# Row maxima written over their scores, score passes that share four banks, and a new order of work in an attention and GEGLU kernel

## The chip, the cores and the metric

The kernel runs on one core of one Trainium2 chip. The metric is the device time of one execution in microseconds, as the median of three runs. The engines are TensorE (PE), VectorE (DVE), ScalarE (ACT), GpSimd (POOL) and the queue of SyncE (SP), which issues all transfers.

## The reference

The input x has 2048 rows of 512. A layer norm, then attention with 32 heads of 16 in four segments of 512 rows, with a compressive memory that is carried from one segment to the next; then a second layer norm and a gated feed-forward with 1376 columns. Cut to what matters:

```python
for s in range(4):                                   # segments of 512 rows
    logits = einsum("bhqd,bhkd->bhqk", qs, ks) * scale + mask
    p = softmax(logits);  a_dot = p @ vs             # mask: -1e9 where the key stands behind the query
    a_mem = (phi(qs) @ M) / (phi(qs) @ z + 1e-6)
    outs.append(g * a_mem + (1 - g) * a_dot)         # g = sigmoid(beta)
    M += phi(ks).T @ vs;  z += phi(ks).sum(rows)
h   = x + concat(outs) @ wo
out = h + (gelu(ln(h) @ w_gate) * (ln(h) @ w_up)) @ w_down
```

All in fp32. The projections are done as three products of high and low parts (`SPLIT`), the softmax with the maximum of each row.

## The kernel before

The order of the work is not that of the Python code. Every instruction is recorded with an engine, a duration, a due time and the values that it reads and writes (`Sched.op`), and `Sched.run` then picks one after another: of those that could start first by its constants, the one with the least due time. `DUE` (L34) holds offsets to the due times, found by a search. `LAT` (L126) is what the planner believes of the time from one engine's result to another's start, `TAKEN` (L132) of the time until a buffer is free. `Pool_` (L54) is a set of buffers; with `fifo` they are given out in the order in which they were asked for, and `then` names the pool that takes them over when nobody waits any more. What the planner picks is fixed in each engine's program; at run time only semaphores hold an instruction back.

The stages are: a prologue (layer norm of the first segments, splitting of weights, the first projections), attention in 16 units of eight heads and one segment, and the feed-forward stage. Each unit is two half units Q of four heads, 32 in all. For each half unit:

- `qkv` (L664) projects q and k (`project`, L610: 4 x 3 products, the low part of xt used by the second of each three), splits them into high and low parts `hl`, and sends these by DMA into the stacked tiles `stq` and `stk`. `phi` (L624) makes `pq` and `pk` for the memory.
- `pass_a` (L785) is for the row maxima. It makes scores with queries on the partitions, for four blocks of 128 queries: 512 and 384 columns (one head to a bank, the wide ones), 256 (two heads to a bank) and 128 (four heads to a bank, the narrow ones). VectorE adds the mask and reduces each head (L807); the elementwise result isn't needed and went to one of two buffers `junk`, the maximum goes to `nm`. The maxima are split in two parts (L823, L826), transposed on PE (L830), copied to `mx` (L833) and sent by DMA into `stq`.
- `pass_b` (L837) makes the scores again with keys on the partitions and the maximum subtracted by the extra rows (L862, L869), takes exp on ScalarE (L876) into `pt`, masks on GpSimd (L879), and accumulates the attention output on PE (L900).

There are eight PSUM banks of 512 columns: three for general use (`PD`), two for the scores of pass A (`PA`), two for those of pass B (`PB`), and one for the accumulation (`PPV`). In the feed-forward stage the last five become `PX` and `PYZ`.

In the prologue `layer_norm` (L455) with `done` keeps PE busy with 17 transposes whose result nobody reads (L497), then transposes the normalised rows (L568) and splits them into high and low parts of xt (L588 on ScalarE, L589 on VectorE). The first unit's two projections are two calls of `project`.

Of the kernel before, what the change touches and what calls it, by code (L numbers as in the profile page):

```python
# [31 lines left out]


DUE = {  # L34
# [17 lines left out]
}  # L52


# [65 lines left out]
class Op:  # L120
# [2 lines left out]

LAT = {  # L126
    "PE": {"PE": 0.0, "ACT": 0.27, "DVE": 0.246, "POOL": 0.24, "SP": 0.25},
    "ACT": {"PE": 0.14, "ACT": 0.12, "DVE": 0.137, "POOL": 0.172, "SP": 0.12},
    "DVE": {"PE": 0.108, "ACT": 0.12, "DVE": 0.17, "POOL": 0.165, "SP": 0.12},
    "POOL": {"PE": 0.085, "ACT": 0.08, "DVE": 0.09, "POOL": 0.12, "SP": 0.12},  # L130
}
TAKEN = {"PE": 0.22, "ACT": 0.14, "DVE": 0.12, "POOL": 0.1}  # L132
DRAIN = 0.1


# [106 lines left out]
def infini_geglu(ctx: ExitStack, tc: tile.TileContext, x, wq, wk, wv, wo, beta,  # L242
# [8 lines left out]
    def sb(name, shape, dt=F32):  # L251
        return p0.tile(shape, dt, name=name)
# [17 lines left out]
        return S.op("POOL", dur, prio, fn, ins, outs, **k)  # L270

    def dma(prio, fn, ins, outs, kb=256, dur=None, **k):
        return S.op("SP", dur or (0.4 if kb == 256 else 0.68), prio, fn, ins, outs, lat=kb / 290, **k)

    def mm(n):
        return max(n / 2400 + 0.0133, 0.109)
# [5 lines left out]
    PD = Pool_(banks[0:3])  # L282
    PX = Pool_([], fifo=True)
    PYZ = Pool_([], fifo=True)
    PA = Pool_(banks[3:5], then=PX)
    PB = Pool_(banks[5:7], then=PYZ)
    PPV = Pool_(banks[7:8], then=PYZ)

    def slots(name, n):
# [21 lines left out]
    PACC = Pool_([], fifo=True)  # L311
    PGE = Pool_(many("ge", 1, [P, D]))
    PC = Pool_([])
    PPT = Pool_(many("pt", 2, [P, D]), then=PACC)
    PROW1 = Pool_(many("pt1", 9, [P, D]), then=PPT)
    PJ = Pool_(many("junk", 2, [P, D]), then=PC)
    PE_ = Pool_(many("e", 1, [P, D]), then=PC)
    PPQ = Pool_(many("pq", 1, [P, D]), then=PC)
    PPK = Pool_(many("pk", 1, [P, D]), then=PC)
    PPKN = Pool_(many("pkn", 1, [P, D]), then=PC)  # L320
    PPVS = Pool_(many("pvs", 1, [P, D]), then=PGE)
# [7 lines left out]
    PMB = Pool_(many("mb", 7, [P, 160]))  # L329
    PNM = Pool_(many("nm", 2, [P, 2, 2, 4]))  # L330
    PMM = Pool_(many("mm", 2, [P, 2, 2, 8], F32R))
    PMX = Pool_(many("mx", 2, [32, P]))
    PBN = Pool_(many("bn", 2, [P, 4, 6]))
    PMV = Pool_(many("mv", 2, [P, 4, 2]))
    PLN = Pool_(many("ln", 8, [P, 4]))

    ident = sb("ident", [P, P])
    amask = sb("amask", [P, D])
# [1 line left out]
    one = sb("one", [P, 1])  # L340
    gt = sb("gt", [P, 2, NCH])
    tick = sb("tick", [P, 1])
    o_dram = dram.tile([NSEG, 4, P, NCH, P], F32, name="o_dram")
    r_dram = dram.tile([16, 2, 8, D], F32, name="r_dram")
    pv_dram = dram.tile([16, 2, P, D], F32, name="pv_dram")
# [2 lines left out]
    vident, vamask, vmmask, vgt = (Val() for _ in range(4))  # L348


    vh = Val(PJ)
    vj = Val(PJ)


# [101 lines left out]
    def layer_norm(prio, rows, dst, off=False, keep=None, acq=None, done=(), behind=(), scratch=None):  # L456
# [37 lines left out]
        if done and not behind:  # L494

            wm = Val(PB)
            pe(17 * 0.227, prio, lambda: [nc.tensor.transpose(  # L497
                wm.t[0:24, 0:P], bn.t.rearrange("p t k -> p (t k)"), ident) for n in range(17)],
                [bn, vident], [wm])

        def g():
# [62 lines left out]
                    op1=OP.mult), [rows[t], mv, y], [rows[t]])  # L564
        if done and not behind:

            pts = [Val(PA if dc == 3 else PD) for dc in range(ND)]
            pe(4 * TR, prio, lambda: [nc.tensor.transpose(  # L568
                pts[dc].t[:, t * P:(t + 1) * P], rows[t].t[:, dc * P:(dc + 1) * P], ident)
                for t in range(4) for dc in range(ND)], [*rows, vident], pts, acq=dst)  # L570
            for dc in range(ND):
                split_psum(prio, pts[dc], dst[dc])
            return
# [47 lines left out]
            pe(3 * mm(D), prio, f, [w, XT[s][dc]], [pm], acq=acq)  # L621
        return pm

    def phi(prio, pm, pool_):  # L624

        e, r = Val(PE_), Val(pool_)
        act(D, prio, lambda: nc.scalar.activation(e.t, pm.t, AF.Relu, scale=-1.0), [pm], [e],
            acq=[r])
        act(D, prio, lambda: nc.scalar.activation(e.t, e.t, AF.Exp, scale=-1.0), [e], [e],
            src=0.092)  # L630
        dve(D, prio, lambda: nc.vector.scalar_tensor_tensor(
            r.t, pm.t, 0.0, e.t, op0=OP.max, op1=OP.add), [pm, e], [r])
        return r
# [31 lines left out]
    def qkv(U):  # L665
# [5 lines left out]
        moved = prio + DUE["d"][U]  # L671
        for Q in half:
            STQ[Q], STK[Q] = Val(PSQ), Val(PSK)
        for i in range(2):
            hl = Val(PHL)
            if U == 0:
                HL0.append(hl)
            pm = project(first + 0.1 * i, W[s // 2, c, i], s, [hl])
            sc = 0.25 if i == 0 else 1.0
            act(D, first, lambda pm=pm, hl=hl, sc=sc: nc.scalar.activation(  # L680
                hl.t[:, 0], pm.t, AF.Copy, scale=sc), [pm], [hl])
            dve(D, first, lambda pm=pm, hl=hl, sc=sc: nc.vector.scalar_tensor_tensor(  # L682
                hl.t[:, 1], pm.t, sc, hl.t[:, 0].bitcast(F32), op0=OP.mult, op1=OP.subtract),
                [pm], [hl])
            if i == 0 and s:
                PQ[U] = phi(first, pm, PPQ)
            if i == 1 and s < NSEG - 1:
                PQ[U, "k"] = phi(first, pm, PPK)
# [94 lines left out]
    def pass_a(Q):  # L783
# [4 lines left out]
        def part(heads, i):  # L788
# [12 lines left out]
            m = mm(2 * w if i < 2 else w)  # L801
            pe(m * len(heads) / 2 if i < 2 else m, prio, f, [sq, sk], [sa], acq=[nm], tail=m)
            for k, (a, p) in enumerate(heads):
                junk = Val(PJ)

                def g(k=k, a=a, p=p, junk=junk):
                    nc.vector.tensor_tensor_reduce(  # L807
                        out=junk.t[:, :w], in0=sa.t[:, k * w:(k + 1) * w], in1=amask[:, D - w:],
                        op0=OP.add, op1=OP.min, scale=-1.0, scalar=BIG,
                        accum_out=nm.t[:, a, p, i:i + 1])  # L810
                dve(w, prio, g, [sa, vamask], [junk, nm], chain=True)
        for i in (3, 2):
            for n in range(4):
                part([(n % 2, n // 2)], i)
# [23 lines left out]
    def pass_b(Q):  # L838
# [55 lines left out]
        def accum(kbs, last):  # L894
            def f():
                for kb in kbs:
                    for n in range(4):
# [7 lines left out]
            pe(sum(0.02 + 0.86 * (4 - kb) / 4 for kb in kbs), Q + 1.122 + DUE["p"][Q], f,  # L905
               [va, *dict.fromkeys(pt[n, kb][0] for kb in kbs for n in range(4))], [pv], head=0.03,
               tail=0.02, mode="c")
        for n in range(4):
# [395 lines left out]
```

## Time and profile before

| | |
|---|---|
| median of 3 runs | 831.09 us (830.61 to 831.82) |
| the profiled execution | 830.79 us, span 829.1 us |
| PE busy | 805.0 us, 97% of the span |
| PE weight load busy | 623.6 us |
| DVE busy | 612.0 us, 74% |
| ACT busy | 563.5 us, 68% |
| POOL busy | 484.2 us, 58% |
| granted clock | 1.000 |

Busy time is the time in which at least one instruction of the engine was under way. Instructions overlap a little, and the ends of matmuls are modelled, so a busy PE is not one that gets all it could do; where it lost time is seen better from the starts of its instructions and from what released them. A row of a group gives busy time and mean duration, then the idle time before its instructions and what ended it. A row of the timeline gives the start, the duration and the instruction.

### The profile page before, as it was taken

To read this page: it belongs to the slowest core of one execution; us is meant where nothing else is said; L and a number is where in the kernel's file an instruction comes from. 1 tells how busy PE (TensorE), PEld (TensorE's weight loads), DVE (VectorE), ACT (ScalarE), POOL (GpSimd) and SP (SyncE) were. 2 spreads that over 40 slices of the span, in tenths; PEclk is the share of its full clock that TensorE was granted. 3 is DMA by queue.
4 is the path that set the end of the run, shared out by engine and by line. 5 is a ranking of instruction groups with operands and counts; after the bars stand their busy time and mean duration, and the time that the engine had idled before them with its cause. 6 is when DMAs were issued, how large, how long until landed. Compare 5 with 4: busy or idle time off the path is not lost.

```text
span 829.1 us, 15346 instructions
## 1 busy us (share of the span) xinstructions
PE 805.0 (97%) x4709; PEld 623.6 (75%) x4709; DVE 612.0 (74%) x1831; ACT 563.5 (68%) x1127; POOL 484.2 (58%) x719
## 2 busy tenths in 40 slices
PE   5999999999999999999999999999999999999998
PEld 4877767777777677776667677777888887788886
DVE  7888678788895878888896874676568856756565
ACT  6877868689988768776776862787467464545551
POOL 7533433444445444544736895788697686778750
PEclk9999999999999999999999999999999999999999
DMA  6543534565456564556554665531111341212102
GB/s 229 148 133 94 153 108 130 151 182 155 118 156 177 159 154 119 154 152 169 165 163 144 200 200 166 164 115 48 55 55 48 95 162 51 65 39 63 51 1 102
DMA packets 71750, 103.52 MB, mean 125 GB/s; under 512 B 14324, under 2 KB 24884, under 8 KB 71668
## 3 DMA queue, kind: packets, MB, share of 16 engines
q1 hardware_dynamic: 71668, 102.54, 42.6%
q8 instruction: 37, 0.61, 0.3%
q14 instruction: 45, 0.37, 0.2%
HBM read 54.92 MB, written 21.43 MB: 92 GB/s over the span
## 4 chain that ended last, share of the span: by engine, by line
PE 77%; DVE 10%; ACT 4%; issue 3%; POOL 3%; DMA 2%; SPq 1%; ACTq 0%; POOLq 0%; DVEq 0%
PE bank L1145 19%; PE bank L1206 14%; PE bank L619 8%; PE bank L797 8%; PE bank L869 7%; PE bank L900 7%; PE bank L973 4%; PE bank L648 4%; DVE junk L807 3%; ACT pt L876 1%; PE bank L726 1%; POOL raw L1122 1%; PE bank L772 1%; PE bank L579 1%; DVE hl L682 1%
## 5 line engine op out<-in xcount | busy, mean ns | idle before, releaser
L807 DVE CUSTOM_DVE_ANT_0 junk<-bank,amask 128x256 f32<-128x256 f32 (+3 forms) x512 | 228.3, 485 | 43.4 <-PE bank L797 40.3
L879 POOL TENSOR_SCALAR_AFFINE_SELECT pt<-pt 128x128 f32<-128x128 f32 (+2 forms) x352 | 118.8, 346 | 191.6 <-ACT pt L876 183.5
L876 ACT ACTIVATE pt<-bank 128x512 f32<-128x512 f32 (+1 forms) x352 | 181.4, 560 | 42.8 <-PE bank L869 36.4
L797 PE MATMUL bank<-stk,stq 128*128 128x512 f32 (+2 forms) x384 | 128.1, 377 | 4.3 <-DVE nm L807 3.9
L869 PE MATMUL bank<-stq,stk 128*128 128x384 f32 (+2 forms) x384 | 110.8, 351 | 1.7 <-ACT pt L876 1.4
L619 PE MATMUL bank<-xt,w 128*128 128x512 f32 x384 | 108.4, 394 | 1.1 <-DVE xt L589 1.1
L1211 DVE TENSOR_TENSOR pt<-pt,bank 128x512 f32<-128x512 f32 x96 | 65.0, 685 | 41.7 <-PE bank L1206 40.1
L797 PEld LDWEIGHTS bank<-stk,stq 128*128 128x128 f32 x384 | 68.6, 188 | 28.4 <-DVE nm L807 13.8
L869 PEld LDWEIGHTS bank<-stq,stk 128*128 128x128 f32 x384 | 67.3, 188 | 19.9 <-ACT pt L876 8.3
L619 PEld LDWEIGHTS bank<-xt,w 128*128 128x128 f32 x384 | 70.4, 188 | 12.5 <-DVE xt L589 1.3
L900 PE MATMUL bank<-pt,vaug 128*32 128x512 f32 (+3 forms) x1024 | 77.0, 436 | 0.0
L900 PEld LDWEIGHTS bank<-pt,vaug 128*32 128x32 f32 x1024 | 28.9, 109 | 39.1 <-issue 30.2
L648 PE MATMUL bank<-wv,xt 128*128 128x256 f32 x384 | 54.9, 283 | 0.0
L648 PEld LDWEIGHTS bank<-wv,xt 128*128 128x128 f32 x384 | 52.2, 189 | 1.8 <-issue 0.2
L1145 PE MATMUL bank<-xt,w 128*128 128x512 f32 (+1 forms) x186 | 51.2, 391 | 0.4 <-DVE n L1171 0.4
L1115 POOL TENSOR_TENSOR w<-raw,w 128x512 fp32r<-128x512 f32 (+3 forms) x37 | 42.0, 1137 | 6.8 <-ACT w L1113 6.6
L435 POOL TENSOR_TENSOR w<-raw,w 128x512 fp32r<-128x512 f32 (+1 forms) x23 | 29.7, 1291 | 22.3 <-ACT w L430 22.1
L807 DVE DVE_READ_ACCUMULATOR2_ANT nm<- 128x1 f32 x512 | 42.0, 82 | 0.0
L1145 PEld LDWEIGHTS bank<-xt,w 128*128 128x128 f32 (+1 forms) x186 | 34.3, 186 | 8.9 <-ACT ge L1163 0.8
L1145 PE MATMUL bank<-stk,w 128*128 128x512 f32 (+1 forms) x138 | 38.8, 390 | 0.0
L1122 POOL TENSOR_TENSOR raw<-raw,raw 128x256 f32<-128x256 f32 (+1 forms) x44 | 35.2, 799 | 2.9
L1122 POOL TENSOR_TENSOR raw<-raw 128x256 f32<-128x256 f32 (+1 forms) x44 | 33.6, 765 | 1.8
(298 smaller groups left out, 1798.5 us busy)
## 6 DMA issues: line engine op xcount, KB each, us to landing
stq<-hl SPq DMA_DIRECT2D x96, 128.0 KB
stk<-hl SPq DMA_DIRECT2D x192, 64.0 KB
pv_dram<-pvs SPq DMA_DIRECT2D x32, 256.0 KB
r<-r_dram SPq DMA_DIRECT2D x28, 256.0 KB
row<-x SPq DMA_DIRECT2D x24, 256.0 KB
raw<-wg SPq DMA_DIRECT2D x20, 256.0 KB
raw<-wu SPq DMA_DIRECT2D x20, 256.0 KB
raw<-wd SPq DMA_DIRECT2D x20, 256.0 KB
```

The source lines that it names most:

```text
L619: nc.tensor.matmul(pm.t, w.t[:, wi, dc * P:(dc + 1) * P], XT[s][dc].t[:, xi, :], start=dc == 0 and n == 0, stop=dc == ND - 1 and n == 2)
L648: nc.tensor.matmul(pm.t[:, 256 * t:256 * t + 256], XT[s][dc].t[:, xi, t0:t0 + P], whl[wi].t[:, h, 256 * (dc % 2):256 * (dc % 2) + 256], st ...
L797: nc.tensor.matmul(sa.t[:, k * w:(k + n) * w].rearrange("x (n w) -> x n w", n=n), sq.t[:, p, i * P:(i + 1) * P], sk.t[:, p, a:a + n, 0:w], ...
L807: nc.vector.tensor_tensor_reduce(out=junk.t[:, :w], in0=sa.t[:, k * w:(k + 1) * w], in1=amask[:, D - w:], op0=OP.add, op1=OP.min, scale=-1 ...
L869: nc.tensor.matmul(sc.t[:, lo:lo + D - q0], sk.t[:, p, a, q0:q0 + P], sq.t[:, p, q0:D], start=True, stop=True)
L876: act(w, prio, lambda: nc.scalar.activation(e.t[:, :w], sc.t[:, :w], AF.Exp), [sc], [e])
L879: nc.gpsimd.affine_select(v, v, pattern=pat + [[1, P]], compare_op=OP.is_ge, fill=0.0, base=0, channel_multiplier=-1)
L900: nc.tensor.matmul(pv.t[32 * n:32 * n + 32, kb * P:D], va.t[:, kb, 17 * j:17 * j + 32], e.t[:, lo:lo + D - kb * P], start=kb == 0, stop=la ...
L1122: pool(0.14 + 2.13e-3 * h, prio, lambda: nc.gpsimd.tensor_tensor(d.t[:, d0:d0 + h], a.t[:, a0:a0 + h], c.t[:, c0:c0 + h], op=o), ins, [d])
L1145: nc.tensor.matmul(dst.t[:w], v.t[:, wi, c0 + j * w:c0 + (j + 1) * w], b[bk][j].t[:, xi, :], start=first and j == 0 and n == 0, stop=j == ...
L1206: nc.tensor.matmul(pm.t, HH[p, f, s][hi].t[:w, t * P:(t + 1) * P], v.t[:w, wi, :], start=f == fl[0] and n == 0, stop=f == fl[-1] and n == 2)
L1211: dve(D, prio, lambda a=a, pm=pm: nc.vector.tensor_tensor(a.t, a.t, pm.t, op=OP.add), [pm], [a])
```

## The change

- `DUE` has new values, from a new search. `LAT` from ACT, DVE and POOL to PE is 0.4 greater, `TAKEN` of ACT and DVE 0.1 greater; the planned durations of the accumulation (L900), of the smaller transfers and of the warm-up are set anew. None of these constants is an instruction.
- `PA` and `PB` are now one pool of four banks, given to whichever pass asks.
- The row maxima of the wide blocks write their elementwise result over the scores in the bank; the narrow ones write it into a new buffer `aside` of 256 columns: both 256-column heads of a bank to the same columns, the 128-column heads to its halves in turn. `junk` (now one buffer) is no longer used by them.
- Buffers: `pq` two instead of one, `mx` one instead of two, `ln` six instead of eight; `pt` is given out in order.
- Prologue: 12 transposes instead of 17; other banks for the first transposes; the first unit's q and k are projected by one function, `project_two`, which uses the high part of xt for four products and the low part for the last two of each six.

```diff
 LAT = {
     "PE": {"PE": 0.0, "ACT": 0.27, "DVE": 0.246, "POOL": 0.24, "SP": 0.25},
-    "ACT": {"PE": 0.14, "ACT": 0.12, "DVE": 0.137, "POOL": 0.172, "SP": 0.12},
-    "DVE": {"PE": 0.108, "ACT": 0.12, "DVE": 0.17, "POOL": 0.165, "SP": 0.12},
-    "POOL": {"PE": 0.085, "ACT": 0.08, "DVE": 0.09, "POOL": 0.12, "SP": 0.12},
+    "ACT": {"PE": 0.54, "ACT": 0.12, "DVE": 0.137, "POOL": 0.172, "SP": 0.12},
+    "DVE": {"PE": 0.508, "ACT": 0.12, "DVE": 0.17, "POOL": 0.165, "SP": 0.12},
+    "POOL": {"PE": 0.485, "ACT": 0.08, "DVE": 0.09, "POOL": 0.12, "SP": 0.12},
 }
-TAKEN = {"PE": 0.22, "ACT": 0.14, "DVE": 0.12, "POOL": 0.1}
+TAKEN = {"PE": 0.22, "ACT": 0.24, "DVE": 0.22, "POOL": 0.1}
...
-    PA = Pool_(banks[3:5], then=PX)
-    PB = Pool_(banks[5:7], then=PYZ)
+    PA = PB = Pool_(banks[3:7], then=Parts(1, PX, PYZ, PX, PYZ))
...
-    PPT = Pool_(many("pt", 2, [P, D]), then=PACC)
+    PPT = Pool_(many("pt", 2, [P, D]), fifo=True, then=PACC)
-    PJ = Pool_(many("junk", 2, [P, D]), then=PC)
+    PJ = Pool_(many("junk", 1, [P, D]), then=PC)
-    PPQ = Pool_(many("pq", 1, [P, D]), then=PC)
+    PPQ = Pool_(many("pq", 2, [P, D]), then=PC)
-    PMX = Pool_(many("mx", 2, [32, P]))
+    PMX = Pool_(many("mx", 1, [32, P]))
-    PLN = Pool_(many("ln", 8, [P, 4]))
+    PLN = Pool_(many("ln", 6, [P, 4]))
+    aside = sb("aside", [P, 2 * P])
...
-            pe(17 * 0.227, prio, lambda: [nc.tensor.transpose(
-                wm.t[0:24, 0:P], bn.t.rearrange("p t k -> p (t k)"), ident) for n in range(17)],
+            pe(12 * 0.21, prio, lambda: [nc.tensor.transpose(
+                wm.t[0:24, 0:P], bn.t.rearrange("p t k -> p (t k)"), ident) for n in range(12)],
...
+    def project_two(prio, w, s, acq):
+        pm = [Val(PD), Val(PD)]
+        for dc in range(ND):
+            def f(dc=dc):
+                for n, (i, wi, xi) in enumerate((i, wi, xi) for wis, xi in (((0, 1), 0), ((0,), 1))
+                                                for i in range(2) for wi in wis):
+                    nc.tensor.matmul(pm[i].t, w[i].t[:, wi, dc * P:(dc + 1) * P], XT[s][dc].t[:, xi, :],
+                                     start=dc == 0 and n in (0, 2), stop=dc == ND - 1 and n > 3)
+            pe(6 * mm(D), prio, f, [*w, XT[s][dc]], pm, acq=acq if dc == 0 else [])
+        return pm
...
-                junk = Val(PJ)
-                def g(k=k, a=a, p=p, junk=junk):
+                def g(k=k, a=a, p=p):
                     nc.vector.tensor_tensor_reduce(
-                        out=junk.t[:, :w], in0=sa.t[:, k * w:(k + 1) * w], in1=amask[:, D - w:],
+                        out=sa.t[:, :w] if i > 1 else aside[:, k * w % 256:k * w % 256 + w], in0=sa.t[:, k * w:(k + 1) * w], in1=amask[:, D - w:],
                         op0=OP.add, op1=OP.min, scale=-1.0, scalar=BIG,
                         accum_out=nm.t[:, a, p, i:i + 1])
-                dve(w, prio, g, [sa, vamask], [junk, nm], chain=True)
+                dve(w, prio, g, [sa, vamask], [nm], chain=True)
```

The rest of the diff is the new values of `DUE`, and the places that pass buffers to the functions above.

More of the change, by code (lines that the diff above doesn't have):

```diff
@@ L272, in dma @@
     def dma(prio, fn, ins, outs, kb=256, dur=None, **k):
-        return S.op("SP", dur or (0.4 if kb == 256 else 0.68), prio, fn, ins, outs, lat=kb / 290, **k)
+        return S.op("SP", dur or (0.4 if kb == 256 else 0.64), prio, fn, ins, outs, lat=kb / 290, **k)
     def mm(n):
@@ L348, in infini_geglu @@
     vident, vamask, vmmask, vgt = (Val() for _ in range(4))
-    vh = Val(PJ)
+    vh = Val(PE_)
     vj = Val(PJ)
@@ L565, in layer_norm @@
         if done and not behind:
-            pts = [Val(PA if dc == 3 else PD) for dc in range(ND)]
+            pts = [Val(pool_) for pool_ in ((PA, PA, PB, PD) if not behind else (PD, PD, PD, PA))]
             pe(4 * TR, prio, lambda: [nc.tensor.transpose(
@@ L622, in project, with phi @@
         return pm
-    def phi(prio, pm, pool_):
-        e, r = Val(PE_), Val(pool_)
+    def project_two(prio, w, s, acq):
[8 more added lines that the diff above has]
+        return pm
+    def phi(prio, pm, r):
+        e = Val(PE_)
         act(D, prio, lambda: nc.scalar.activation(e.t, pm.t, AF.Relu, scale=-1.0), [pm], [e],
@@ L673, in qkv @@
             STQ[Q], STK[Q] = Val(PSQ), Val(PSK)
+        hls = Val(PHL), Val(PHL)
+        if U == 0:
+            first_two = project_two(first, [W[0, 0, 0], W[0, 0, 1]], 0, hls)
         for i in range(2):
-            hl = Val(PHL)
+            hl = hls[i]
             if U == 0:
                 HL0.append(hl)
-            pm = project(first + 0.1 * i, W[s // 2, c, i], s, [hl])
+            if i == 0 and s:
+                PQ[U] = Val(PPQ)
+            if i == 1 and s < NSEG - 1:
+                PQ[U, "k"] = Val(PPK)
+            r = PQ.get((U, (U, "k"))[i])
+            pm = project(first + 0.1 * i, W[s // 2, c, i], s, [hl] + ([r] if r else [])) if U else first_two[i]
             sc = 0.25 if i == 0 else 1.0
@@ L684, in qkv @@
                 [pm], [hl])
[L685 to L688, printed above, removed]
+            if r:
+                phi(first, pm, r)
             for h, Q in enumerate(half):
@@ L904, in f @@
                                          tile_position=(0, 32 * n), skip_group_check=True)
-            pe(sum(0.02 + 0.86 * (4 - kb) / 4 for kb in kbs), Q + 1.122 + DUE["p"][Q], f,
+            pe(sum(0.735 * (4 - kb) / 4 for kb in kbs) + (0.17 if last else 0.06), Q + 1.122 + DUE["p"][Q], f,
                [va, *dict.fromkeys(pt[n, kb][0] for kb in kbs for n in range(4))], [pv], head=0.03,
```

33 rows, old and new, of the table DUE are left out of this document.

## The prediction

> **What bounds the kernel now.** I read the page's engine rows and chain first, then busy time by stretch, then the waits, then single stretches of the timeline.
>
> ```profile
> span 829.1 us, 15346 instructions
> PE 805.0 (97%) x4709; PEld 623.6 (75%) x4709; DVE 612.0 (74%) x1831; ACT 563.5 (68%) x1127; POOL 484.2 (58%) x719
> PE 77%; DVE 10%; ACT 4%; issue 3%; POOL 3%; DMA 2%; SPq 1%; ACTq 0%; POOLq 0%; DVEq 0%
> ```
>
> TensorE (PE) is busy nearly throughout and carries 77% of the chain. But the ends of matmuls are modelled, so I count starts instead. The chain that ended last, in order of time, has undisturbed stretches of each kind of product:
>
> ```profile
> 42.66 0.71 PE bank L648 x6
> 56.64 2.29 PE bank L900 x32
> 601.84 12.26 PE bank L1145 x54
> ```
>
> A 512-column product takes 12.26/54 = 0.227 us, a 256-column one 0.71/6 = 0.118, the 32 matmuls of one accumulation of attention outputs 2.29. All PE instructions laid end to end at such spacings make about 772 us (an estimate from these rows; the 384-column products by interpolation). The other 57 us of the span are stalls, and that is all that a new order can win. Where are they?
>
> ```profile
> 28.00:480.00 452.00, 442.42 (x3078) 329.64 (x3076) 366.96 (x1406) 355.24 (x743) 216.96 (x441) 1.00 0.53 150
> 480.00:829.10 349.10, 343.78 (x1519) 278.25 (x1517) 223.07 (x363) 189.61 (x353) 246.56 (x235) 1.00 0.28 85
> 28.00:480.00 452.00, 230.33 (x1024) 1.00 0.53 150
> ```
>
> The columns are PE, weight load, DVE (VectorE), ACT, POOL. In the attention stage (28 to 480) VectorE is busy 366.96 of 452 us, 81%; in the feed-forward stage 64%, and PE is full there. The third row is the row maxima of pass A alone (L807): 230.33/32 = 7.2 us of VectorE for each of the 32 passes. What PE waits for in the attention stage:
>
> ```profile
> DVE junk L807 <- PE bank L797: 40.3, 66, 3.2
> PEld bank L797 <- DVE nm L807: 13.8, 32, 1.7
> PEld bank L869 <- ACT pt L876: 8.3, 24, 1.0
> PE bank L797 <- DVE nm L807: 3.9, 8, 0.8
> ```
>
> The last three are PE or its weight load held by a bank that VectorE or ScalarE has not given back: 13.8 + 8.3 + 3.9 = 26 us. VectorE in turn waits 40.3 us for scores. So the two engines are coupled through few banks, and what slows VectorE in pass A reaches PE.
>
> **The change, part by part.** I laid the two built programs' instruction orders, with their waits, side by side. Each engine but PE has the same number of instructions; PE has five less (the warm-ups). Nothing but the order, the buffers and the waits changes, so every term is a stall won or lost. The profiled execution took 830.79 us, 829.1 of it the span, with a median of 831.09; I sum against 830.8.
>
> *Prologue.*
>
> ```profile
> 7.61 3.58 PE L497 MATMUL bank<-ident,bn 128*24 128x128 f32 x17 [7.61 <-DVE bn L491]
> 10.55 0.64 PE L497 MATMUL bank<-ident,bn 128*24 128x128 f32 x3
> 11.02 1.91 PE L568 MATMUL bank<-ident,pt 128*128 128x128 f32 x16
> 14.02 0.96 PE L619 MATMUL bank<-xt,w 128*128 128x512 f32 x3 [1.08 <-DVE xt L589]
> 9.80 1.45 DVE L533 TENSOR_SCALAR pt<-pt,mv,ln 128x512 f32<-128x512 f32 x3
> 12.64 2.07 ACT L588 ACTIVATE xt<-bank 128x512 fp32r<-128x512 f32 x4 [1.91 <-PE bank L568]
> ```
>
> The first projection starts at 14.02, held 1.08 us for the low part of xt from VectorE. In the new order its first four products need only the high part, which ScalarE has about 0.6 us after 12.64 (a quarter of 2.07, and its tail). Five warm-ups less free PE earlier, but the third normalised row is ready only at 9.80 + 1.45 = 11.25, so that gives half a microsecond at most. I take -1.1; the ends are -1.6 (both in full) and +1.6. The upper end is the clock: the last three warm-ups stand (11.02-10.55)/3 = 0.16 us apart, the 14 before them (10.55-7.61)/14 = 0.21. So the array sped up near the end of 17; after 12 it may not have, and 16 transposes at 0.21 in place of 0.11 cost 1.6. The Trainium skill says the same ("TensorE: Matmul & The Clock Gate", Part 1): the clock is released after some 3.4 us of sustained work, in a free-running window. Twelve at 0.21 us end before that, so by the page the +1.6 is the likelier; the trace of before cannot decide.
>
> *Row maxima: wide ones over their scores, narrow ones in one buffer.* The output of a wide one moves from SBUF to the bank it reads. The nearest rows are one operation of VectorE with either output:
>
> ```profile
> L1157 DVE TENSOR_TENSOR bank<-vaug,bank 128x512 f32<-128x512 f32 x22 | 15.2, 693 | 11.7 <-PE bank L1145 8.4 <-ACT vaug L1152 3.2
> L1157 DVE TENSOR_TENSOR vaug<-vaug,bank 128x512 f32<-128x512 f32 x9 | 6.2, 687 | 1.3 <-PE bank L1145 1.3
> ```
>
> 6 ns more for each of 256 wide maxima is at most 1.5 us on VectorE, at least 0; I take 0.8.
>
> The 256 narrow ones are the costly part. Before, two buffers took turns; now both 256-column heads of a bank write the same 256 columns of `aside`. The new order therefore has 125 narrow maxima (94 of the 256-column ones, 31 of the 128-column ones) that wait for the maximum directly ahead of them on VectorE itself: 65 for that alone, 60 for another engine too. Before there were 7, all with a second wait. What such a wait costs is in the trace:
>
> ```profile
> 180.28 0.69 DVE L807 CUSTOM_DVE_ANT_0 junk<-bank,amask 128x512 f32<-128x512 f32 x1
> 180.89 0.08 DVE L807 DVE_READ_ACCUMULATOR2_ANT nm<- 128x1 f32 x1
> 181.12 0.69 DVE L807 CUSTOM_DVE_ANT_0 junk<-bank,amask 128x512 f32<-128x512 f32 x1
> ...
> 208.00 0.69 DVE L807 CUSTOM_DVE_ANT_0 junk<-bank,amask 128x512 f32<-128x512 f32 x1
> 208.62 0.69 DVE L807 CUSTOM_DVE_ANT_0 junk<-bank,amask 128x512 f32<-128x512 f32 x1
> ...
> 212.17 0.69 DVE L631 SCALAR_TENSOR_TENSOR pq<-bank,e 128x512 f32<-128x512 f32 x1
> 212.78 0.34 DVE L936 RECIPROCAL cd<-cd 128x32 f32<-128x32 f32 x1
> 213.16 0.59 DVE L937 TENSOR_SCALAR cd<-cd,gt 128x32 f32<-128x32 f32 x1
> ```
>
> At 208 two maxima without the wait start 0.62 us apart. At 180 the second has it, and PE's too, and starts 0.84 after the first: 0.22 more. A single wait is seen at L937, which needs L936: it starts 0.04 after its end, where L936, without a wait, starts 0.08 before the end of L631: 0.12 more. So 60 x 0.22 + 65 x 0.12 - 7 x 0.22 = 19.5 us more on VectorE, 0.61 a pass. Behind the waiting instruction stand the rest of the pass's maxima, their split and their copy, and the banks that they hold; for those PE waits.
>
> How much reaches PE? Between nothing (VectorE idles 452 - 367 = 85 us in this stage) and all 19.5. In the new order the two passes hardly interleave: from a pass A product to a pass B product, or back, PE changes 63 times instead of 393. In 20 of the 32 passes the products of pass A now stand within less PE work than the 7.2 us that VectorE needs for their maxima (before: in none); there VectorE sets the pace, and nothing hides a longer tail. I take 20/32 of 19.5: +12.2.
>
> *Order, margins, four shared banks, the new due times.* The planner now believes that PE hears of the other engines 0.4 us later and lets either pass take any of four banks. Counting at the spacings above, PE work between a product and the next wait for what VectorE, ScalarE or GpSimd made of it is short of their durations in 140 of 1319 waits before and in 223 of 1442 after (self-waits left out), while the median room in the attention stage grows from 0.50 to 0.67 us. More waits with room, but more short ones. Ends: -26, if the margins remove every wait in the rows above; and, at 26/140 = 0.19 us a short wait, 83 more at +16. The two signs nearly cancel; I lean to the count and take +3.
>
> *The rest.* One buffer less for mx makes its copy on VectorE wait for the transfer of the pass before; behind it stand the next pass's maxima. By the new order the transposes ahead of these copies are at least 5.5 us of PE work apart, median 12, so the transfer is long over: 0, and a fraction of a microsecond in the closest pair. The second pq buffer frees a product that nothing in the waits above names: 0. Fewer ln buffers: 0, off the path. Feed-forward order: the second stretch has PE at 98%; 0, within 2 either way (inside the range of the order).
>
> Sum: 830.8 - 1.1 + 0.8 + 12.2 + 3 = 845.7, say **846**.
>
> **The rivals.**
> - *The order wins.* Four banks and margins halve the 26 us of waits, and the self-waits fall into VectorE's 85 idle us. 830.8 - 1.1 - 13 = 817. For it: waits with room are commoner. Against it: the passes now follow each other, so VectorE's idle time is no longer in pass A. It decides if PE's waits for L807's successor fall below half of 17.7 (13.8 + 3.9).
> - *Self-waits are free.* The mechanism: the maximum behind the wait starts 0.62 us after the one ahead, as at 208. Then 830.8 - 1.1 + 0.8 + 3 = 833.5. The Trainium skill ("VectorE: DVE Perf Modes", "The DRAIN you can't avoid") has eight copies take the same time with a semaphore after each as with one at the end. The rows at 180 and 213 speak against it, but they are few.
> - *VectorE becomes the bound of attention.* All 19.5 us are paid, and the short waits cost their 16: 830.8 - 1.1 + 1.5 + 19.5 + 16 = 867. For it: in the new order little other PE work lies inside a pass A. Against: in 12 passes some does.
>
> **How the numbers follow.** Forecast 0.58, order wins 0.16, self-waits free 0.12, VectorE the bound 0.14. A measurement here can tell about 0.2% (1.7 us) from no change. Faster by more: 0.16 and 0.02 of the free case, 0.18. Within: 0.05 of the free case. Slower: 0.05 of it, 0.58 and 0.14, 0.77. The forecast's own ends, with the order between -8 and +12, are 835 to 855; the range goes down to 828 and up to 863, leaving out most of the first rival and the upper half of the last.
>
> **What would show it.** Two 256-column maxima of before, without the wait:
>
> ```profile
> 101.37 0.42 DVE L807 CUSTOM_DVE_ANT_0 junk<-bank,amask 128x256 f32<-128x256 f32 x1
> 101.72 0.42 DVE L807 CUSTOM_DVE_ANT_0 junk<-bank,amask 128x256 f32<-128x256 f32 x1
> ```
>
> Right: these pairs, at L823 in the new kernel, 0.12 to 0.22 us further apart than 101.72 - 101.37 = 0.35; waits of pass A and pass B products for VectorE well above 17.7 us together; the feed-forward stage about as long as before; the first projection near 13 us. Wrong: narrow maxima as close as before (self-waits free), or PE's waits for VectorE below 10 us (the order wins). A first projection at 14 or later would show the slow clock in the prologue.

## The result, and the profile after

The changed kernel takes 842.37 us (842.00 to 843.54, four runs) against 831.12 us for the kernel before beside it: a ratio of 1.0139, with a 95% interval from 1.0123 to 1.0155. It is slower by 11.25 us, 1.4%. The profiled execution has a span of 840.3 us and a granted clock of 0.998.

The page of the changed kernel, its engine rows and its chain:

```profile
span 840.3 us, 15312 instructions
PE 816.0 (97%) x4704; PEld 623.7 (74%) x4704; DVE 620.8 (74%) x1831; ACT 556.5 (66%) x1127; POOL 483.1 (57%) x719
PE 75%; DVE 19%; issue 2%; ACT 2%; DMA 1%; SPq 0%; DVEq 0%; POOL 0%; ACTq 0%; POOLq 0%
PE bank L1161 24%; PE bank L1222 14%; PE bank L885 7%; DVE bank L823 7%; PE bank L619 6%; PE bank L916 6%; PE bank L815 5%; PE bank L989 5%; DVE aside L823 5%; PE bank L660 3%; PE bank L579 1%; PE bank L790 1%; DVE nm L823 1%; DVE hl L702 1%; DVE ln L515 1%
```

The busy shares say almost nothing: 97% for PE as before. The chain does: VectorE's share went from 10% to 19%, and 13% of it (7 + 5 + 1) is one line, L823, the row maxima (L807 before). Their narrow form, `aside`, stands on the path by itself with 5%. (A release by a semaphore is inferred, so a share of the chain is a pointer; the experiments below decide.)

Where in the span was the time lost? The last product with `wo` closes the attention stage. In order, its row in the timeline of before, of after, and of `two12_same`, which is told below:

```profile
536.64 0.84 PE L973 MATMUL bank<-xt,wv 128*128 128x512 f32 x3
```

```profile
550.45 0.84 PE L989 MATMUL bank<-xt,wv 128*128 128x512 f32 x3
```

```profile
534.86 0.84 PE L989 MATMUL bank<-xt,wv 128*128 128x512 f32 x3
```

Attention ends 13.8 us later than before. What comes behind it takes 829.1 - 537.5 = 291.6 us before and 840.3 - 551.3 = 289.0 after, so the feed-forward stage gave 2.6 us back.

The waits of the changed kernel (who waited for whom: us in total, times, the longest), cut to PE and its weight load held by VectorE or ScalarE:

```profile
PEld bank L885 <- DVE nm L823: 16.2, 38, 0.8
PEld bank L815 <- DVE nm L823: 15.5, 42, 1.6
...
PEld bank L885 <- ACT pt L892: 5.8, 18, 0.7
...
PE bank L815 <- DVE nm L823: 3.5, 5, 1.3
PE bank L885 <- DVE nm L823: 2.9, 12, 0.3
```

PE now waits 16.2 + 15.5 + 3.5 + 2.9 = 38.1 us for the maxima, against 17.7 before. Half of it is new in kind: L885 is pass B, and its products before (L869) waited for no maxima at all. Since the four banks are shared, a pass B product can take a bank that pass A's maxima still hold.

The forms of the maxima, out of the groups of before and then of after:

```profile
L807 DVE CUSTOM_DVE_ANT_0 junk<-bank,amask 128x512 f32<-128x512 f32 x128 | 85.9, 683 | 13.1 <-PE bank L797 12.3
...
L807 DVE CUSTOM_DVE_ANT_0 junk<-bank,amask 128x256 f32<-128x256 f32 x128 | 48.0, 420 | 5.3 <-PE bank L797 4.5
L807 DVE DVE_READ_ACCUMULATOR2_ANT nm<- 128x1 f32 x512 | 42.0, 82 | 0.0
```

```profile
L823 DVE CUSTOM_DVE_ANT_0 bank<-bank,amask 128x512 f32<-128x512 f32 x128 | 85.9, 712 | 21.0 <-PE bank L815 20.7
...
L823 DVE DVE_READ_ACCUMULATOR2_ANT nm<- 128x1 f32 x512 | 56.7, 111 | 0.0
L823 DVE CUSTOM_DVE_ANT_0 aside<-bank,amask 128x256 f32<-128x256 f32 x128 | 54.1, 423 | 9.6 <-PE bank L815 3.2
```

The 256-column form hardly takes longer itself (423 against 420 ns), yet its busy time rose from 48.0 to 54.1 us: instructions that used to overlap no longer do, and its idle time before it, 5.3 before, is 9.6 with only 3.2 put down to PE.

### The profile page after: what moved, and what is told of

Read it like the earlier page. It is cut to its first block, busy times and chain, and to the rows that moved or that the text cites. A ratio compares the mean times of both kernels' runs of the same rounds, so it can differ in the third digit from the quotient of the medians.

```text
span 840.3 us, 15312 instructions
## 1 busy us (share of the span) xinstructions
PE 816.0 (97%) x4704; PEld 623.7 (74%) x4704; DVE 620.8 (74%) x1831; ACT 556.5 (66%) x1127; POOL 483.1 (57%) x719
## 4 chain that ended last, share of the span: by engine, by line
PE 75%; DVE 19%; issue 2%; ACT 2%; DMA 1%; SPq 0%; DVEq 0%; POOL 0%; ACTq 0%; POOLq 0%
PE bank L1161 24%; PE bank L1222 14%; PE bank L885 7%; DVE bank L823 7%; PE bank L619 6%; PE bank L916 6%; PE bank L815 5%; PE bank L989 5%; DVE aside L823 5%; PE bank L660 3%; PE bank L579 1%; PE bank L790 1%; DVE nm L823 1%; DVE hl L702 1%; DVE ln L515 1%
## 5 line engine op out<-in xcount | busy, mean ns | idle before, releaser
L892 ACT ACTIVATE pt<-bank 128x512 f32<-128x512 f32 (+1 forms) x352 | 171.5, 572 | 23.1 <-PE bank L885 20.1
L823 DVE CUSTOM_DVE_ANT_0 bank<-bank,amask 128x512 f32<-128x512 f32 (+1 forms) x256 | 153.1, 649 | 34.2 <-PE bank L815 33.8
L815 PE MATMUL bank<-stk,stq 128*128 128x512 f32 (+2 forms) x384 | 112.5, 381 | 4.3 <-DVE nm L823 3.5
L885 PE MATMUL bank<-stq,stk 128*128 128x384 f32 (+2 forms) x384 | 108.6, 368 | 4.0 <-DVE nm L823 2.9
L619 PE MATMUL bank<-xt,w 128*128 128x512 f32 x360 | 103.0, 396 | 0.0
L823 DVE CUSTOM_DVE_ANT_0 aside<-bank,amask 128x256 f32<-128x256 f32 (+1 forms) x256 | 83.7, 355 | 16.1 <-PE bank L815 5.0
L815 PEld LDWEIGHTS bank<-stk,stq 128*128 128x128 f32 x384 | 67.2, 189 | 29.8 <-DVE nm L823 15.5
L885 PEld LDWEIGHTS bank<-stq,stk 128*128 128x128 f32 x384 | 64.0, 188 | 31.5 <-DVE nm L823 16.2
L823 DVE DVE_READ_ACCUMULATOR2_ANT nm<- 128x1 f32 x512 | 56.7, 111 | 0.0
L435 POOL TENSOR_TENSOR w<-raw,w 128x512 fp32r<-128x512 f32 (+1 forms) x27 | 35.3, 1309 | 35.7 <-ACT w L430 29.2
L1131 POOL TENSOR_TENSOR w<-raw,w 128x512 fp32r<-128x512 f32 (+2 forms) x34 | 40.3, 1188 | 7.8 <-ACT w L1129 7.2
L1131 POOL TENSOR_TENSOR stk<-raw,stk 128x512 fp32r<-128x512 f32 (+3 forms) x26 | 28.9, 1115 | 23.1 <-ACT stk L1129 16.0
L937 ACT ACTIVATE pvs<-bank 128x512 f32<-128x512 f32 x32 | 19.1, 596 | 28.7 <-PE bank L916 16.8
```

The costliest lines, as they stand in the source:

```text
L619: nc.tensor.matmul(pm.t, w.t[:, wi, dc * P:(dc + 1) * P], XT[s][dc].t[:, xi, :], start=dc == 0 and n == 0, stop=dc == ND - 1 and n == 2)
L815: nc.tensor.matmul(sa.t[:, k * w:(k + n) * w].rearrange("x (n w) -> x n w", n=n), sq.t[:, p, i * P:(i + 1) * P], sk.t[:, p, a:a + n, 0:w], ...
L823: nc.vector.tensor_tensor_reduce(out=sa.t[:, :w] if i > 1 else aside[:, k * w % 256:k * w % 256 + w], in0=sa.t[:, k * w:(k + 1) * w], in1= ...
L885: nc.tensor.matmul(sc.t[:, lo:lo + D - q0], sk.t[:, p, a, q0:q0 + P], sq.t[:, p, q0:D], start=True, stop=True)
L892: act(w, prio, lambda: nc.scalar.activation(e.t[:, :w], sc.t[:, :w], AF.Exp), [sc], [e])
L1131: pool(0.14 + 2.13e-3 * (hi - lo), prio, lambda: nc.gpsimd.tensor_tensor(v.t[:, 1, :hi - lo], r.t[:, lo:hi], v.t[:, 0, :hi - lo].bitcast(F ...
```

## The experiments

Three theories. A: the time went into the **self-waits**, the narrow maxima that wait for the maximum directly ahead because both write the same columns of `aside`. B: it went into the **new order** itself, the passes one behind the other on shared banks. C: it went into the **wide outputs in PSUM**, over the scores. Each ratio is to the kernel before on the same chip, and has its 95% interval.

**1. The new kernel without self-waits (`a_narrow_two`).** The buffer keeps its 1 KB, but holds all 512 columns in two bytes, so neighbouring heads write different columns. No engine's order changes; the 125 self-waits become 0.

```diff
-    aside = sb("aside", [P, 2 * P])
+    aside = sb("aside", [P, D], mybir.dt.bfloat16)
...
-  out=sa.t[:, :w] if i > 1 else aside[:, k * w % 256:k * w % 256 + w], ...
+  out=sa.t[:, :w] if i > 1 else aside[:, k * w:k * w + w], ...
```

> The changed kernel in its own order, every instruction at its place, but the four narrow maxima of a pass write to buffers that take turns (bf16 in the same 1 KB, values that nobody reads), so that none waits for the one directly ahead: 125 self-waits become 0. Theory A (the self-waits on VectorE set the new time): 256-column maxima go back from 0.47 and 0.58 us apart to 0.35, VectorE has 20 us less to do, PE's waits for VectorE fall, and the kernel takes 830 to 834 us. Theory B (the new order and the shared banks cost the time, the self-waits fall into idle time of VectorE): 839 to 842.5 us. If the outputs in PSUM are what costs (theory C): 838 to 842.

829.87 us, ratio 0.9960 (0.9946 to 0.9974). The whole loss is gone; the time is just below theory A's range. I ran it again beside the changed kernel on one chip (`two12_same` and `after_same`, below).

**2. The old kernel with self-waits (`b_narrow_aside`).** The same order as before, but the narrow maxima write one `aside`, in two bytes as well, so it is not the narrower type that makes experiment 1 fast; one `ln` buffer less makes room, and no wait for `ln` grew by more than 0.2 us. In it 112 narrow maxima wait for the one directly ahead, 62 of them for that alone.

```diff
-    PLN = Pool_(many("ln", 8, [P, 4]))
+    PLN = Pool_(many("ln", 7, [P, 4]))
...
+    aside = sb("aside", [P, 2 * P], mybir.dt.bfloat16)
...
-  out=junk.t[:, :w], ...
+  out=junk.t[:, :w] if i > 1 else aside[:, k * w % 256:k * w % 256 + w], ...
```

> The kernel of before in its own order, but its narrow maxima write to one buffer aside, as the change has them (bf16, and one ln buffer less to make room), which gives 112 self-waits, 62 alone and 50 with a second wait: 62 x 0.12 + 50 x 0.23 = 19 us more on VectorE. Theory A: the old order interleaves the passes and hides more of it, but not all: 834 to 842 us. Theory B: 831 to 832.5.

839.34 us, ratio 1.0080 (1.0066 to 1.0095). The waits of this kernel:

```profile
PEld bank L797 <- DVE nm L807: 19.3, 46, 1.7
...
PE bank L797 <- DVE nm L807: 4.8, 13, 0.8
```

19.3 + 4.8 = 24.1 us against 17.7: 6.4 us more, and 0.80% of 832.5 is 6.7 us. So self-waits alone make the old kernel slower, but by less: in the old order, where the passes interleave, about a third of their 19 us reaches the end (5.5 to 7.9 us by the interval).

**3. The old kernel with wide outputs in PSUM (`b_wide_over`).**

```diff
-  out=junk.t[:, :w], ...
+  out=sa.t[:, :w] if i > 1 else junk.t[:, :w], ...
```

> The kernel of before in its own order, but its wide maxima write over their scores in PSUM. In the changed kernel the next instruction after such a maximum starts 0.04 us later (0.648 instead of 0.609 for 512 columns, 0.515 instead of 0.475 for 384), which would be 256 x 0.04 = 10 us on VectorE. Theory C (that is a good part of the lost time): 834 to 838 us. Theories A and B: 830 to 833.

832.80 us, ratio 1.0002 (0.9993 to 1.0012). Theory C falls for this order. The output in PSUM isn't free on VectorE, as this kernel's groups show:

```profile
L807 DVE CUSTOM_DVE_ANT_0 bank<-bank,amask 128x512 f32<-128x512 f32 x128 | 87.4, 699 | 13.3 <-PE bank L797 13.0
...
L807 DVE DVE_READ_ACCUMULATOR2_ANT nm<- 128x1 f32 x512 | 56.8, 111 | 0.0
```

699 against 683 ns, and 111 against 82 ns for the reading of the accumulator; in the time none of it shows, to within about 1 us.

**4. The warm-up (`a_warm17`).** The changed kernel with 17 warm-ups.

```diff
-  ... for n in range(12)],
+  ... for n in range(17)],
```

> The changed kernel with 17 warm-up transposes instead of 12, all else in place. In its profile the granted clock reached full speed 1.2 us later after the start than before, and the 16 transposes that follow took 2.63 us instead of 1.91. If the shorter warm-up costs the prologue's gain: 1 to 2 us faster, 840.5 to 841.5. If the prologue's end is set by the layer norm of the second segment on VectorE anyway: 842 to 843.

841.13 us, ratio 1.0098 (1.0080 to 1.0116). That is inside the range for a warm-up that matters, but the changed kernel itself has 1.0139, 1.0087 and 1.0119 in three sets of runs, so this doesn't tell 12 from 17.

**5. The changed kernel again (`after_again`, `after_same`).** No edit, to have it beside the others.

> The changed kernel unaltered, on the same chip as the next three, so that they can be set against it: 1.4% above before, by the first measurement (1.012 to 1.016).

> The changed kernel unaltered once more, as the base of this chip for the next three: ratio to before 1.007 to 1.016, the span of the two measurements so far.

838.81 us, ratio 1.0087 (1.0071 to 1.0104), and 842.07 us, ratio 1.0119 (1.0102 to 1.0136). The first lies below what was expected, and its interval does not reach that of the first measurement (1.0123 to 1.0155). So only kernels on one chip are subtracted below.

Part of this scatter is the array's clock. All four executions of the first measurement had a granted clock of 0.998; of the six of `after_again` four had 1.000. The profile of the changed kernel shows what 0.998 stands for: one stretch of 3.4 us at half clock. First that stretch, then the two products of L790 in it, then the same two in `a_warm17`, whose profile has no such stretch (a row of a stretch gives its length, the busy time of PE, weight load, DVE, ACT and POOL, the granted clock, and the share and rate of DMA):

```profile
230.50:233.90 3.40, 3.40 (x10) 1.58 (x14) 3.02 (x19) 2.78 (x4) 0.00 (x1) 0.50 0.91 218
```

```profile
231.73 1.91 PE L790 MATMUL bank<-pq,mb 128*128 128x512 f32 x2
```

```profile
231.36 1.02 PE L790 MATMUL bank<-pq,mb 128*128 128x512 f32 x2
```

Behind this stretch the changed kernel is 1.4 us later than `a_warm17`, and ahead of it 0.1 us earlier: 1.5 us for one such stretch. It follows 3.5 us (227.0 to 230.5) in which PE was busy for only 2.13, most of the rest a wait for VectorE's maxima. `a_warm17` has the same wait without such a stretch behind it, so the wait alone doesn't bring it on. Three of the four profiles with self-waits in the new order have one such stretch between the prologue and the last few microseconds, and none of the five without them. The executions without self-waits are not free of lower clocks either (0.995 to 1.000 in `two12_same`), so how much of the loss goes this way isn't priced.

**6. On one chip: the self-waits, the warm-up, the PSUM outputs (`two12_same`, `two17_same`, `sbuf17`).** The first is `a_narrow_two` again, the second has 17 warm-ups as well. The third also takes the wide outputs out of PSUM: all maxima write bytes that nobody reads into two 512-byte buffers in turn, in the same order and without self-waits.

```diff
+    aside_t = sb("aside", [P, 2, D], mybir.dt.uint8); aside = (aside_t[:, n % 2] for n in range(512))
...
+  out=next(aside)[:, :w], ...
```

> The changed kernel with narrow maxima in buffers that take turns, 12 warm-up transposes, beside the unaltered one on the same chip. Theory A (about two thirds or more of the 20 us of self-waits reach the end): 11 to 16 us below the unaltered one.

> The same with 17 warm-up transposes. If the longer warm-up saves 1 to 3 us: below the one with 12 by 0.1 to 0.4%. If the release of the clock depends on more than the number of warm-ups: no difference beyond 0.1%.

> As the one before (17 warm-ups, no self-waits), but all maxima, wide ones too, write to two buffers in SBUF that take turns (8-bit values that nobody reads, to fit the room). If the outputs over the scores cost what the rows of the changed kernel seem to show (0.04 us after some wide maxima, at most 256 x 0.04 = 10 us on VectorE): 2 to 7 us faster than the one before. If that is hidden, as in the kernel of before: within 1 us.

| on the same chip | us | ratio | interval |
|---|---|---|---|
| before | 831.98 | | |
| `after_same` | 842.07 | 1.0119 | 1.0102 to 1.0136 |
| `two12_same` | 828.03 | 0.9959 | 0.9941 to 0.9978 |
| `two17_same` | 827.31 | 0.9947 | 0.9930 to 0.9964 |
| `sbuf17` | 826.79 | 0.9940 | 0.9918 to 0.9962 |

The self-waits cost 842.07 - 828.03 = 14.0 us, give or take 2 by the two intervals. On two other chips the nearest pairs have 17 warm-ups on one side: 838.81 - 826.51 = 12.3 (`after_again`, `two_warm17`) and 841.13 - 829.87 = 11.3 (`a_warm17`, `a_narrow_two`). So it is 11 to 14 us. Here are some narrow maxima in the timeline of the changed kernel, and then some in `two12_same` (start, duration, instruction):

```profile
60.86 0.42 DVE L823 CUSTOM_DVE_ANT_0 aside<-bank,amask 128x256 f32<-128x256 f32 x1
61.21 0.08 DVE L823 DVE_READ_ACCUMULATOR2_ANT nm<- 128x1 f32 x1
61.33 0.42 DVE L823 CUSTOM_DVE_ANT_0 aside<-bank,amask 128x256 f32<-128x256 f32 x1
61.67 0.08 DVE L823 DVE_READ_ACCUMULATOR2_ANT nm<- 128x1 f32 x1
61.90 0.42 DVE L823 CUSTOM_DVE_ANT_0 aside<-bank,amask 128x256 f32<-128x256 f32 x1
```

```profile
71.49 0.42 DVE L823 CUSTOM_DVE_ANT_0 aside<-bank,amask 128x256 bf16<-128x256 f32 x1
71.84 0.09 DVE L823 DVE_READ_ACCUMULATOR2_ANT nm<- 128x1 f32 x1
71.84 0.42 DVE L823 CUSTOM_DVE_ANT_0 aside<-bank,amask 128x256 bf16<-128x256 f32 x1
```

With the self-wait 61.33 - 60.86 = 0.47 us from one to the next, and 61.90 - 61.33 = 0.57 where a second wait stands beside it; without it 71.84 - 71.49 = 0.35. VectorE's share of the chain is back at that of before:

```profile
PE 85%; DVE 10%; ACT 2%; DMA 2%; issue 1%; SPq 0%; POOL 0%; ACTq 0%; POOLq 0%
```

And PE, in the waits of `two12_same`:

```profile
PEld bank L815 <- DVE nm L823: 11.6, 35, 1.6
...
PEld bank L885 <- ACT pt L892: 5.8, 20, 0.7
...
PEld bank L885 <- DVE nm L823: 5.2, 15, 0.4
...
PEld bank L916 <- POOL pt L895: 3.8, 13, 0.4
...
PE bank L815 <- DVE nm L823: 2.2, 5, 1.3
```

For the maxima 11.6 + 5.2 + 2.2 = 19.0 us in place of 38.1. Pass B's part fell from 16.2 + 2.9 to 5.2, so the new waits of pass B were mostly the self-waits handed on through the shared banks.

The wide outputs, in the new order: VectorE's busy time at L823 from 28 to 480 us, in `two12_same` and in `sbuf17`:

```profile
28.00:480.00 452.00, 228.02 (x1024) 1.00 0.54 152
```

```profile
28.00:480.00 452.00, 218.72 (x1024) 1.00 0.54 152
```

9.3 us of VectorE for 0.5 us between the medians (827.31 in `two17_same` to 826.79, with the same 17 warm-ups), where the intervals are about 1.5 us either way. Theory C falls here too, but for 1 or 2 us at most. Twelve or 17 warm-ups can't be told apart (828.03 and 827.31).

**7. 17 warm-ups on another chip (`two17_same` first as `two_warm17`).**

> The changed kernel with its narrow maxima in buffers that take turns, and 17 warm-up transposes instead of 12. If the longer warm-up saves what it seemed to save on the changed kernel (0.4%): ratio to before 0.991 to 0.994, about 3 us below the one with 12. If it only moves the prologue by the 1.2 us of the clock's later release, and that is hidden behind the second layer norm: 0.995 to 0.997, as with 12.

826.51 us, ratio 0.9941 (0.9924 to 0.9957). The interval reaches into both expectations, so this doesn't settle the warm-up either. The version without self-waits is faster than both kernels on every chip that it ran on.

**8. The margins (`two_nomargin`).** `a_narrow_two` with the latencies of before, and the new due times.

```diff
-    "ACT": {"PE": 0.54, ...      "DVE": {"PE": 0.508, ...      "POOL": {"PE": 0.485, ...
+    "ACT": {"PE": 0.14, ...      "DVE": {"PE": 0.108, ...      "POOL": {"PE": 0.085, ...
-TAKEN = {"PE": 0.22, "ACT": 0.24, "DVE": 0.22, "POOL": 0.1}
+TAKEN = {"PE": 0.22, "ACT": 0.14, "DVE": 0.12, "POOL": 0.1}
```

> The changed kernel with its narrow maxima in buffers that take turns, and with the planner's latencies of before (the margins of 0.4 and 0.1 us gone); the due times stay as the change has them, so the order differs. If the margins make the order robust: PE's waits for VectorE and ScalarE grow, 833 to 840 us. If they matter little once the self-waits are gone: 828 to 832. The due times were found with the margins, so a slower result bounds their worth from above.

872.36 us, ratio 1.0492 (1.0472 to 1.0512): far outside both expectations. Its waits:

```profile
DVE bank L823 <- PE bank L815: 55.6, 36, 12.5
...
POOL n L958 <- DMA r<-r_dram: 35.6, 5, 24.8
```

Single waits of 12 and 25 us are no margin of 0.4 us that is missing; they are another order, in which long chains end late. The due times were found with the latencies that they stand with, and don't carry over. The granted clock was 0.983 as well, with 29 us of the span at half clock, so part of the loss may be a slower array. This run doesn't price the margins.

**9. The sharing (`b_shared`).** The kernel before with the shared pool and `pt` in order, its own due times and latencies.

```diff
-    PA = Pool_(banks[3:5], then=PX)
-    PB = Pool_(banks[5:7], then=PYZ)
+    PA = PB = Pool_(banks[3:7], then=Parts(1, PX, PYZ, PX, PYZ))
...
+    PPT = Pool_(many("pt", 2, [P, D]), fifo=True, then=PACC)
```

> The kernel of before with one part of the change alone: four banks shared by both passes (and pt given out in order, without which no order is found), with the old due times, latencies and outputs. The new order then changes between the passes 51 times instead of 393, as in the changed kernel (63), so it is the sharing that makes the passes follow each other. If following each other costs by itself (VectorE idle in pass B, ScalarE in pass A): 838 to 850 us. If it is neutral and the change's loss was the self-waits alone: 828 to 836.

899.13 us, ratio 1.0806 (1.0783 to 1.0828), outside both expectations, and by the most of all. Its waits:

```profile
DVE junk L807 <- PE bank L797: 72.8, 30, 10.1
...
PEld bank L797 <- DVE nm L807: 30.5, 82, 0.8
```

PE changes between the passes 51 times here, as rarely as in the changed kernel (63), against 393 before. So the passes one behind the other come with the shared pool (and `pt` in order), without the new search. With due times that don't fit it this order costs 8%. Some of that may be a slower array and not waiting: the granted clock was 0.969, with 56 us of the span behind the prologue at half clock against none before, and the run doesn't separate the two. How much of the new kernel's order is owed to the sharing, to the search, and to the margins stays open: the three only work together, and no run separates them.

## Why the prediction was right, point by point

The time came out at 842.4, forecast 846, inside the range; slower had the largest chance. The pairs of narrow maxima and PE's waits (38.1 us against 17.7) came as its signs said. The nearness of the sum is in part luck: the self-waits were put too low and the rest had the wrong sign, and the two errors partly cancel.

*Self-waits, +12.2: the mechanism and its size hold.* Over all pairs of 256-column maxima, the median from start to start is 0.345 us without the wait, 0.466 with it alone and 0.577 with a second (the first in `two12_same`, the others in the changed kernel): 0.12 and 0.23 more, forecast 0.12 and 0.22. If the 128-column ones cost the same, the 125 self-waits are 65 x 0.121 + 60 x 0.232 = 21.8 us on VectorE, forecast 21.0 (19.5 with the old ones taken off). 14.0 of them reached the end: 64%, against 20/32 = 62%. With 11 to 14 us it is 52% to 64%, so that the two agree this closely is chance, and where an execution has the half-clock stretch, 1.5 us of the loss is that. That the share comes from the passes standing apart is in line with `b_narrow_aside`, though the two orders differ in more than this: 62 x 0.121 + 50 x 0.232 = 19.1 us, of which 6.7, 35%, reached the end in the interleaved order. Why it is 64% and not some other share in the new order was counted from the order, not shown by a run. The rival in which self-waits are free is out, and so is the one in which all of them are paid. The kernel before has many 256-column maxima that wait for an earlier instruction of VectorE which is not the one directly ahead, since its two `junk` take turns. Those start 0.345 us apart, so it is the wait for the one directly ahead that costs. The Trainium skill ("VectorE: DVE Perf Modes", "The DRAIN you can't avoid") has eight copies take the same time with a semaphore after each as with one at the end. For waits on earlier instructions this case's traces agree; for waits on the one directly ahead they do not (0.12 us more), and there the measurement decides.

*Order, margins, shared banks, +3: this is the term that failed, in sign.* Without the self-waits the new kernel is at 828.03 against 831.98, so all else together is -4.0. By the rows of the last `wo` product, attention ends 1.8 us earlier in `two12_same` than before, and 0.5 of that is that its first data came earlier (7.15 in its first row, which is shown last, against 7.61); the feed-forward stage took 824.8 - 535.7 = 289.1 us, 2.5 less than before. The feed-forward part is firm: it is 288.8 to 289.6 us in all nine profiles of the new order, with self-waits or without, and 291.6 to 292.2 in the three of the old one. I had put it at nothing within 2. The rest, a microsecond or so, lies inside what one execution differs from the next.

I had weighed the count of short waits (+16) against the room of the others (-26) and leaned to the count. The rows don't show either at such a size. Without self-waits PE's waits for the maxima are 19.0 us, not less than the 17.7 before; its waits for `pt` fell a little, for ScalarE from 8.3 to 5.8 us and for GpSimd from the 7.0 of this row of before to 3.8:

```profile
PEld bank L900 <- POOL pt L879: 7.0, 28, 0.4
```

The rival in which the order wins was right about the order's sign, but wrong about its size (-13) and its mechanism, since it had PE's waits for the maxima halved.

*Prologue, -1.1: the wait went as said, but what it is worth depends on the clock.* The changed kernel's PE in the prologue (in brackets, idle time and what ended it):

```profile
7.89 2.72 PE L497 MATMUL bank<-ident,bn 128*24 128x128 f32 x12 [7.89 <-DVE bn L491]
10.68 2.63 PE L568 MATMUL bank<-ident,pt 128*128 128x128 f32 x16
13.66 5.73 PE L631 MATMUL bank<-xt,w 128*128 128x512 f32 x24 [0.36 <-ACT xt L588]
19.23 6.22 PE L660 MATMUL bank<-wv,xt 128*128 128x256 f32 x48
25.63 1.60 PE L579 MATMUL bank<-ident,pt 128*128 128x128 f32 x4 [0.17 <-DVE pt L533]
```

The first projection starts at 13.66, waiting 0.36 us for ScalarE's high part in place of 1.08 for VectorE's low one, as the step said. But the 16 transposes took 2.63 us in place of 1.91: the array was still slow after 12 warm-ups, which I had as the upper end of the term and not as its value. My sign for that, a first projection at 14 or later, missed it. And what was left of the gain ended at L579, whose input comes from the layer norm on VectorE (L533). `a_warm17` shows that: its transposes took 1.91 us, and its L579 stands at 25.65 all the same.

The profile of before, though, is one in which the array sped up early. The same prologue, with its 17 warm-ups, was slow in the three other profiles that have it, for example `b_wide_over`, whose first row starts at 7.54:

```profile
11.12 3.08 PE L568 MATMUL bank<-ident,pt 128*128 128x128 f32 x16
```

```profile
26.63 1.51 PE L579 MATMUL bank<-ident,pt 128*128 128x128 f32 x4
```

From the first row to L579 that is 26.63 - 7.54 = 19.09 us, and 18.8 and 18.9 in the other two. The profile of before has 17.7, the new prologue 17.4 to 18.5, whatever its clock. So the new one gains nothing to 0.3 us where the array is fast, and about 1 us where it is slow. No run has the prologue's change alone.

*Wide outputs, +0.8: right as a sum, for another reason.* On VectorE they cost 9 us and not 1.5, since the reading of the accumulator also grew (82 to 111 ns on average over all 512, half of which have an output in PSUM). But none of it was seen at the end, within about 1 us by `b_wide_over` and 2 by `sbuf17`.

*The sum* is 14.0 - 4.0 = +10.0 on the chip of the table, and was forecast as +14.9: the difference is 6.7 us for the sign of all that isn't a self-wait (forecast +2.7), less the 1.8 by which the self-waits were put too low.

## What to carry to other kernels

A buffer that nobody reads still orders its writers: give such scratch outputs at least two places in turn, or the engine waits for itself wherever an instruction writes where the one directly ahead of it wrote. How much of a stall on one engine reaches the end depends on what stands beside it: self-waits cost a third of their time where the passes interleaved and half to two thirds where they stood one behind the other. Due times that a search found hold only with the latencies and pools that they were found with, so a single one of these taken out measures another order, not its own worth.

## What the runs showed of the hardware that was not expected

- On VectorE an instruction that waits for nothing starts before the one ahead of it has ended (0.42 us long, 0.35 us apart in `two12_same`); with a wait for that one it starts after its end (0.47 apart), and with a second wait later still (0.57). A wait for an earlier one costs nothing (0.345 us apart in the kernel before).
- A maximum whose elementwise result goes to PSUM makes its accumulator's reading longer: 0.14 us, against 0.08, in this stretch of the changed kernel's timeline, where the narrow one behind has its result in SBUF:

```profile
59.83 0.60 DVE L823 CUSTOM_DVE_ANT_0 bank<-bank,amask 128x384 f32<-128x384 f32 x1
60.35 0.14 DVE L823 DVE_READ_ACCUMULATOR2_ANT nm<- 128x1 f32 x1
```

- The point at which the array speeds up is not set by the number of warm-ups. The first rows of `two12_same` and of `two17_same`:

```profile
7.15 2.72 PE L497 MATMUL bank<-ident,bn 128*24 128x128 f32 x12 [7.15 <-DVE bn L491]
9.94 2.20 PE L568 MATMUL bank<-ident,pt 128*128 128x128 f32 x16
```

```profile
7.66 3.79 PE L497 MATMUL bank<-ident,bn 128*24 128x128 f32 x17 [7.66 <-DVE bn L491]
11.24 2.41 PE L568 MATMUL bank<-ident,pt 128*128 128x128 f32 x16
```

The 16 transposes took 2.20 us behind 12 warm-ups and 2.41 behind 17. Over all profiles they took 2.20 to 3.34 us behind 12 (six profiles) and 1.91 to 3.08 behind 17 (eight), and the granted clock became full 2.7 to 6.0 us after the first warm-up. That agrees with the free-running window of the Trainium skill ("TensorE: Matmul & The Clock Gate", Part 1). With such a spread a few runs can't price the warm-up.

- The array can fall back to half clock in the middle of a kernel: in the profile of the changed kernel once, for 3.4 us, which made it 1.5 us later; in that of `b_shared` for 56 us of the span.
